# An attention and FFN kernel in split fp32: q and k laid out turned by the host, raw words as the high part

## The chip, the cores and the metric

The kernel runs on one core of a Trainium2 chip. The metric is the device time of one execution in microseconds (us), the median of several runs. The engines are named as in the profile: PE is the matrix engine (PEld its weight loads), DVE the vector engine, ACT the scalar engine, POOL the general engine, SP the engine whose queue issues the DMA transfers.

## The reference

Block-sparse attention over 4 x 8 heads with 768 positions of 64 columns, and then an FFN over the 3072 tokens of 512 columns:

```
scores = (q @ k.T) / sqrt(D)            # per head, 768 x 768
mask   = |blk_i - blk_j| <= 1, first and last block rows and columns,
         and 3 sampled key blocks of 32 for each query block
attn   = softmax(where(mask, scores, -1e9));   x = attn @ v
h = x @ w_in;   g = h - tanh(h);   out = g @ w_out
```

All inputs and the output are fp32.

## The kernel before

Every fp32 operand of a product on PE is taken as a sum of two parts, a high part that PE multiplies exactly and a low part that is the difference. Two heads form a pair (pr = 0 to 15; head h is half j = h % 2 of pair h // 2). The operands of a pair lie in one of three slots in SBUF (slot = pr % 3), each 128 x 4 x 2 x 768 words: sA, sB, sC, sD for x = 0 to 3, and the two halves j. The rows of sA hold the high part of k and the block mask, sB the high part of q, the one-hot block rows and (row 88) the negated row maximum nm, sC the low and high part of k, sD the high and low part of q.

For a pair, `load` brings k, q and v (rawk, rawq, rawv, 384 KB each, two buffers each). `prep_qk` turns k, and then q, by six 128 x 128 transposes on PE (L198) into a PSUM buffer, copies the result as the high part with ACT (hik, hiq, L200) and subtracts on DVE for the low part (lok, loq, L201). hi and lo have one buffer each. `dist` brings them into the slot by twelve transfers of 192 KB (L213): half j = 0 and j = 1 of k high into sA and sC, k low into sC, q high into sB and sD, q low into sD. A transfer into half j may start when the head that used this half of the slot, three pairs earlier, has been read for the last time.

For each head there are six steps over blocks of 128. `smax` (sm, L255) takes an estimate of the scores of 128 queries and DVE reduces it to a maximum (mc, L259). `smax_fin` turns the maxima (pmt, L264), forms nm on DVE (L266) and sends it into sB. `qk_exp` forms the scores turned, 128 keys x 768 queries (st, L283 and L284), and ACT takes the exponential (pe, L287). `split` makes its fp16 high part (ph, ACT L297 or DVE L295) and low part (pl, POOL L299, one of twelve on DVE). `accum` multiplies them by the parts of v (av, L313, L321, L322, 36 products for two key blocks), `norm` divides (xq, L335) and `spill` stores a pair's x in DRAM. sm, st and the turned q and k share the three PSUM buffers of the pool `big`, in rotation.

All steps are put in a list of events with a time each (`at`), sorted by it, and emitted in that order; a scheduler with a model of the engines then sets the order in which each engine has its instructions, and the buffers set the waits. SP issues its transfers strictly in that order, at most eight under way. In the first 150 us three pairs of FFN weight blocks are also read and converted on DVE (L436, L439, L442). The FFN follows: x and the weights are split in the same way, `h` and `out` are products on PE.

Of the kernel before, what the change touches and what calls it, by code (L numbers as in the profile page):

```python
# [55 lines left out]
TQK, TV, TSM, LSP, LAV = -15.1, -5.6, -9.95, 2.1, 4.2  # L56
# [16 lines left out]


@with_exitstack
def attention_ffn(ctx, tc, q, k, v, samp, w_in, w_out, blocks, out):
    nc = tc.nc
    cst = ctx.enter_context(tc.tile_pool(name="cst", bufs=1))
    dpool = ctx.enter_context(tc.tile_pool(name="dpool", bufs=1, space=DRAM))
    xscr = [dpool.tile([P, T, DM], F32, name=f"xscr{b}") for b in range(B)]  # L80

    ident = cst.tile([P, P], F32, name="ident")
    make_identity(nc, ident)
    bias = [cst.tile([P, 1], F32, name=f"bias{i}") for i in range(2)]
    for x, val in zip(bias, (QB, THR2)):
        nc.vector.memset(x, val)

    slots = [cst.tile([P, 4, 2, S], F32R, name=f"slot{i}") for i in range(NSLOT)]
    wt = {(m, ft): dpool.tile([P, 512], F32, name=f"w{m}{ft}") for ft in range(NPRE) for m in "io"}
    part = [dpool.tile([P, DM], F32, name=f"part{j}") for j in range(CT)]  # L90
    f2 = ctx.enter_context(tc.tile_pool(name="f2", bufs=2))
    stage = [cst.tile([P, 1024], I32, name=f"stage{i}") for i in range(2)]
    ffn = FFN(tc, w_in, w_out, xscr, ident, bias, slots, wt, out, f2, part, stage)
    with ExitStack() as actx:
        big = actx.enter_context(tc.tile_pool(name="ps_big", bufs=3, space=PSUM))
        one = actx.enter_context(tc.tile_pool(name="ps_one", bufs=2, space=PSUM))
        ps = (
            lambda name: big.tile([P, 1024], F32, tag="big", name=name),
            lambda name: one.tile([P, 512], F32, tag="one", name=name),
        )  # L100
        ffn.big, ffn.one = ps
        attention(actx, tc, q, k, v, samp, w_in, w_out, blocks, xscr, ident, ps, slots, wt, f2, ffn)
    with ExitStack() as fctx:
        ffn.rest(fctx)


def attention(ctx, tc, q, k, v, samp, w_in, w_out, blocks, xscr, ident, ps, slots, wt, f2, ffn):
    nc = tc.nc
# [9 lines left out]
    loads = {}  # L118
# [16 lines left out]
    def after(n, d):  # L135
        for f in urgent[n]:
            tc.add_manual_dep(
                d.ins, f.ins.name, mybir.DependencyInfo(mybir.DependencyClass.NoSync, mybir.DependencyReason.DATA), reason="first pair"
            )

    def load(pr, which="kqv", first=None):
        r = loads.setdefault(pr, [])
        for nm, src in ((n, x) for n, x in (("k", k), ("q", q), ("v", v)) if n in which):
            t = p2.tile([P, S], F32, tag="raw" + nm, name=f"raw{nm}{pr}", bufs=2)
            d = nc.sync.dma_start(out=t, in_=src[pr])
            r.append(t)
            if pr <= 3 and first is not None:
                after(first, d)

    load(0, "kq")  # L150
# [38 lines left out]
    hl = {}  # L189
    sbs = {}  # L190

    def prep_qk(pr, nm):
        raw = loads[pr][0 if nm == "k" else 1]
        hi = p2.tile([P, S], F32R, tag="hi" + nm, name=f"hi{nm}{pr}", bufs=1)
        lo = p2.tile([P, S], F32R, tag="lo" + nm, name=f"lo{nm}{pr}", bufs=1)
        pt = big(f"pt{nm}{pr}")
        for t in range(T):
            nc.tensor.transpose(pt[:, t * P : (t + 1) * P], raw[:, t * P : (t + 1) * P], ident)  # L198
        ptv = pt[:, 0:S]
        nc.scalar.activation(out=hi, in_=ptv, func=AF.Copy)  # L200
        nc.vector.tensor_tensor(out=lo, in0=ptv, in1=hi.bitcast(F32), op=ALU.subtract)  # L201
        hl[pr, nm] = hi, lo

    def dist(pr, nm, part):
        s = pr % NSLOT
        hi, lo = hl[pr, nm]
        if nm == "k":
            to = ((sA, 0, hi),) if part == 0 else ((sC, 64, hi), (sC, 0, lo))
        else:
            to = ((sB, 0, hi),) if part == 0 else ((sD, 0, hi), (sD, 64, lo))  # L210
        for dst, r0, src in to:
            for j in range(2):
                d = nc.sync.dma_start(out=dst[s].bitcast(F32)[r0 : r0 + 64, j], in_=src.bitcast(F32)[64 * j : 64 * j + 64])  # L213
                if pr == 0:
                    urgent[part].append(d)

    def prep_v(pr):
        rv = loads[pr][2]
        vf = rv.rearrange("p (n d) -> p n d", d=D)
        am = p2.tile([P, 1], F32, tag="am", name=f"am{pr}")  # L220
        d = nc.vector.tensor_reduce(
            out=am, in_=rv, op=ALU.max, axis=AX.X, apply_absolute_value=True
        )
        if pr > 1:
            tc.add_manual_dep(
                d.ins, maxed[-1].ins.name, mybir.DependencyInfo(mybir.DependencyClass.NoSync, mybir.DependencyReason.DATA), reason="late"
            )
# [118 lines left out]
    def ramp(h, by):  # L346

        return by * max(0, 1 - (h - 1) / HR) if h else 0

    def at(time, f, *args):  # L350
        ev.append((time, len(ev), f, args))

    at(-17.0, fill, 0, sB, onehot)
    at(TQK + 0.3, fill, 0, sA, mask, 0)
    at(TQK + 0.9, load, 1, "kq", 0)
    at(TQK + 1.7, load, 0, "v", 1)
    for i in range(1, NSLOT):
        for dst, src in ((sB, onehot), (sA, mask)):
            at(TQK + TF * i, fill, i, dst, src, 1)
    for pr in range(NPAIR):  # L360
        t0 = 12 * pr
        tl = TSM + ramp(NMH - 1, RS) + 6 * NMH + 0.1 * pr
        tqk, tv = TQK + ramp(2 * pr, RQ), TV + ramp(2 * pr, RV)
        if pr == 1:
            at(tl, load, 1, "v", 2)
        elif pr:
            at(max(t0 - 30, tl), load, pr, "kqv", 2)
        for nm, dt in (("k", 0), ("q", 0.5)):
            at(t0 + tqk + dt, prep_qk, pr, nm)
# [28 lines left out]
    xa = x_parts(slots[(NPAIR - 3) % NSLOT].rearrange("p a j s -> p (a j s)"))  # L398

    def x_first(j):  # L400
        raw = p2.tile([P, DM], F32, tag="raw" + "kq"[j % 2], name=f"xn0_{j}", bufs=2)
        nc.sync.dma_start(out=raw, in_=xscr[0][:, j, :])
        if j % 2 == 0:
            xa.append(big(f"xt0_{j}"))
        pt = xa[-1][:, j % 2 * 512 : j % 2 * 512 + 512]
        split_x(nc, raw, pt, xa[0][:, :, j * P : (j + 1) * P], xa[1][:, :, j * P : (j + 1) * P], ident)

    for j in range(CT):
        at(X0 + DX * j, x_first, j)
# [38 lines left out]
def split_x(nc, src, pt, xh, xl, ident):  # L448

    for c in range(NCT):  # L450
        nc.tensor.transpose(pt[:, c * P : (c + 1) * P], src[:, c * P : (c + 1) * P], ident)  # L451
    ptv = pt.rearrange("p (c n) -> p c n", c=NCT)
    nc.scalar.activation(out=xh, in_=ptv, func=AF.Copy)
    nc.vector.tensor_tensor(out=xl, in0=ptv, in1=xh.bitcast(F32), op=ALU.subtract)
# [230 lines left out]
```

## Time and profile before

| | |
|---|---|
| runs, us | 983.65, 980.24, 983.49; median 983.49 |
| span of the profiled execution, us | 983.2 (its own time is not listed apart) |
| busy: PE, DVE, ACT, POOL | 94%, 75%, 64%, 47% |
| transfers over the span | 99.78 MB, mean 101 GB/s |
| attention, about | 0 to 450 us |
| FFN, about | 450 to 983 us |

The page has each engine's busy time, the span in 40 slices with the busy share in tenths (PEclk is the granted clock of PE in tenths of full), the chain of work that ended last, and the costliest groups of instructions with what released them. Rows of single instructions give the start, the duration, the engine, the line, and in brackets how long the engine was idle ahead and what it waited for. The chain of waits gives start, duration and what was running.

### The profile page before, as it was taken

The page shows a single profiled execution, that of the slowest core. Times are in us where ns is not written, and L with a number is a line of the kernel's source. Part 1 is how long each engine was busy: PE and PEld are TensorE (multiplying, and loading weights), DVE is VectorE, ACT ScalarE, POOL GpSimd, SP SyncE. Part 2 cuts the span into 40 slices and gives each one's busy share as a digit, 9 for nine tenths or more (in the row PEclk, how much of TensorE's full clock was granted, in tenths as well). Part 3 has the DMA queues.
Part 4 walks back from the last instruction along what each step waited for, and adds up shares of the span by engine and source line. Part 5 has one row for each costly group of instructions (what it writes and reads, how often), then busy time and mean ns, then how long its engine had stood idle before and what let it go on. Part 6 is the DMA issues. An engine that isn't in the chain of part 4 may idle for free.

```text
span 983.2 us, 18548 instructions
## 1 busy us (share of the span) xinstructions
PE 922.6 (94%) x7264; PEld 771.1 (78%) x7264; DVE 733.4 (75%) x1119; ACT 629.7 (64%) x943; POOL 458.3 (47%) x308
## 2 busy tenths in 40 slices
PE   5788999999999999888999999999999999999997
PEld 3577788887888878767788888888888888888885
DVE  4589888887887878859999876765676666566664
ACT  1476888888888878656666665555555465555553
POOL 1365877777777777754445422222222222222221
PEclk9698999999999999898999999999999999999999
DMA  8796777676676667114451220210020000001001
GB/s 231 185 274 190 195 175 175 162 174 162 168 173 162 162 161 189 45 48 157 148 168 50 65 76 11 97 33 12 1 75 1 1 33 11 1 1 44 1 1 43
DMA packets 56263, 99.78 MB, mean 101 GB/s; under 512 B 6008, under 2 KB 26680, under 8 KB 56176
## 3 DMA queue, kind: packets, MB, share of 16 engines
q1 hardware_dynamic: 56176, 98.60, 37.0%
q8 instruction: 57, 0.93, 0.4%
q14 instruction: 30, 0.25, 0.1%
HBM read 44.64 MB, written 15.20 MB: 61 GB/s over the span
## 4 chain that ended last, share of the span: by engine, by line
PE 77%; ACT 6%; DMA 5%; DVE 5%; issue 3%; SPq 1%; POOL 1%; ACTq 0%; POOLq 0%; DVEq 0%
PE pf L537 25%; PE pf L569 8%; PE pf L570 8%; PE pf L571 8%; PE st L283 6%; PE st L284 5%; PE sm L255 5%; ACT pe L287 3%; PE av L313 2%; PE av L321 2%; PE av L322 2%; DMA slot<-lok 2%; DMA slot<-nm 2%; DVE mc L259 1%; PE pf L451 1%
## 5 line engine op out<-in xcount | busy, mean ns | idle before, releaser
L299 POOL TENSOR_TENSOR pl<-pe,ph 128x768 f16<-128x768 f32 x173 | 290.0, 1692 | 130.5 <-ACT ph L297 67.5
L560 POOL TENSOR_TENSOR gl<-t,gh 128x512 fp32r<-128x512 f32 x96 | 124.0, 1292 | 358.4 <-ACT gh L559 307.0
L259 DVE TENSOR_REDUCE mc<-sm 128x1 f32<-128x768 f32 x192 | 181.0, 951 | 53.1 <-PE sm L255 49.2
L287 ACT ACTIVATE pe<-st 128x768 f32<-128x768 f32 x192 | 154.1, 805 | 78.4 <-PE st L284 68.5
L283 PE MATMUL st<-slot 128*128 128x512 f32 (+1 forms) x384 | 146.4, 382 | 17.1 <-ACT pe L287 13.4
L552 DVE TENSOR_TENSOR t<-t,pf 128x512 f32<-128x512 f32 x94 | 64.5, 686 | 123.3 <-ACT t L546 123.2
L559 ACT ACTIVATE gh<-t 128x512 fp32r<-128x512 f32 x96 | 60.6, 632 | 120.2 <-DVE t L556 120.2
L297 ACT ACTIVATE ph<-pe 128x768 f16<-128x768 f32 x154 | 130.0, 844 | 4.7
L284 PE MATMUL st<-slot 89*128 89x512 f32 (+1 forms) x384 | 126.1, 349 | 1.0 <-DMA slot<-nm 1.0
L313 PE MATMUL av<-vhl,ph 128*128 128x65 f16 x1152 | 120.7, 195 | 0.0
L322 PE MATMUL av<-vhl,pl 128*128 128x65 f16 x1152 | 119.6, 194 | 0.9 <-POOL pl L299 0.9
L255 PE MATMUL sm<-slot 88*128 88x512 f32 (+1 forms) x384 | 111.1, 376 | 9.6 <-DMA slot<-hiq 7.0
L321 PE MATMUL av<-vhl,ph 128*128 128x64 f16 x1152 | 119.7, 196 | 0.0
L313 PEld LDWEIGHTS <-ph 128*128 128x128 f16 x1152 | 106.6, 97 | 13.6 <-issue 12.9
L322 PEld LDWEIGHTS <-pl 128*128 128x128 f16 x1152 | 107.9, 100 | 3.0 <-issue 1.5
L321 PEld LDWEIGHTS <-ph 128*128 128x128 f16 x1152 | 107.9, 98 | 0.7 <-issue 0.5
L544 ACT ACTIVATE u<-pf 128x512 f32<-128x512 f32 x94 | 56.2, 598 | 80.5 <-PE pf L537 80.2
L283 PEld LDWEIGHTS st<-slot 128*128 128x128 f32 x384 | 74.9, 195 | 35.1 <-ACT pe L287 18.5
L284 PEld LDWEIGHTS st<-slot 89*128 89x128 f32 x384 | 75.5, 197 | 11.2 <-DMA slot<-nm 2.2
L255 PEld LDWEIGHTS sm<-slot 88*128 88x128 f32 x384 | 62.6, 202 | 17.0 <-DMA slot<-mk 6.3
L570 PE MATMUL pf<-wx,gh 128*128 128x512 f32 x192 | 74.7, 389 | 0.0
L569 PE MATMUL pf<-wx,gh 128*128 128x512 f32 x192 | 74.7, 389 | 0.0
(123 smaller groups left out, 1962.8 us busy)
## 6 DMA issues: line engine op xcount, KB each, us to landing
slot<-hik SPq DMA_DIRECT2D x64, 192.0 KB
slot<-hiq SPq DMA_DIRECT2D x64, 192.0 KB
stage<-w_in SPq DMA_DIRECT2D x13, 512.0 KB
stage<-w_out SPq DMA_DIRECT2D x13, 512.0 KB
rawk<-k SPq DMA_DIRECT2D x16, 384.0 KB
rawq<-q SPq DMA_DIRECT2D x16, 384.0 KB
slot<-lok SPq DMA_DIRECT2D x32, 192.0 KB
slot<-loq SPq DMA_DIRECT2D x32, 192.0 KB
```

The source lines that it names most:

```text
L255: nc.tensor.matmul(pm[:, c], lhsT=sB[s][0:88, j, t * P : (t + 1) * P], rhs=sA[s][0:88, j, c], start=True, stop=True)
L259: maxed.append(nc.vector.tensor_reduce(out=mcs[h][:, t : t + 1], in_=pm[:, 0:S], op=ALU.max, axis=AX.X))
L283: ms.append(nc.tensor.matmul(st[:, c], lhsT=sC[s][:, j, kc], rhs=sD[s][:, j, c], start=True, stop=False))
L284: ms.append(nc.tensor.matmul(st[:, c], lhsT=sA[s][0:89, j, kc], rhs=sB[s][0:89, j, c], start=False, stop=True))
L287: nc.scalar.activation(out=pe, in_=st[:, 0:S], func=AF.Exp, scale=0.125)
L299: d = eng.tensor_tensor(out=pl, in0=pe, in1=ph, op=ALU.subtract)
L313: m = nc.tensor.matmul(o[:, t, :], lhsT=ph[:, c], rhs=vv[:, 0:65], start=(kt == 0 and t == 0), stop=False, skip_group_check=True)
L321: nc.tensor.matmul(o[:, t, 0:64], lhsT=ph[:, c], rhs=vv[:, 65:129], start=False, stop=False, skip_group_check=True)
L322: m = nc.tensor.matmul(o[:, t, :], lhsT=pl[:, c], rhs=vv[:, 0:65], start=False, stop=last, skip_group_check=True)
L537: nc.tensor.matmul(h, lhsT=w[:, cc], rhs=x[:, c, :], start=(k == 0), stop=(k == 3 * NCT - 1))
L569: nc.tensor.matmul(o, lhsT=gh[:, c], rhs=wo[0][ft], start=(ft == f0), stop=False)
L570: nc.tensor.matmul(o, lhsT=gh[:, c], rhs=wo[1][ft], start=False, stop=False)
```

## The change

The host lays out k and q of a pair turned and side by side, in one array of 16 x 128 x 1536 (row 64 j + d, column 768 x + position, x = 0 for k). One load (rawx, 768 KB, two buffers) takes the place of two. The transposes and the copies on ACT go. The high parts go into the slots straight from rawx, as raw words. For the low part DVE forms the words with the last 12 bits cleared (hi, L196, 128 x 1536) and subtracts these from the raw words (lo, L197, 128 x 1536), each with one buffer. The twelve transfers of a pair into the slot remain (now L210). The times of the events are altered so that the transfers of the high parts stand ahead of `prep_qk`. Four tiles of x at the start of the FFN take the buffers of rawv.

```diff
 def load(pr, which="kqv", first=None):
-    r = loads.setdefault(pr, [])
-    for nm, src in ((n, x) for n, x in (("k", k), ("q", q), ("v", v)) if n in which):
-        t = p2.tile([P, S], F32, tag="raw" + nm, name=f"raw{nm}{pr}", bufs=2)
-        d = nc.sync.dma_start(out=t, in_=src[pr])
+    for nm, src, n in (("x", kq, 2 * S), ("v", v, S)):
+        if nm in which:
+            t = p2.tile([P, n], F32, tag="raw" + nm, name=f"raw{nm}{pr}", bufs=2)
+            d = nc.sync.dma_start(out=t, in_=src[pr])
...
-def prep_qk(pr, nm):
-    raw = loads[pr][0 if nm == "k" else 1]
-    hi = p2.tile([P, S], F32R, tag="hi" + nm, name=f"hi{nm}{pr}", bufs=1)
-    lo = p2.tile([P, S], F32R, tag="lo" + nm, name=f"lo{nm}{pr}", bufs=1)
-    pt = big(f"pt{nm}{pr}")
-    for t in range(T):
-        nc.tensor.transpose(pt[:, t * P : (t + 1) * P], raw[:, t * P : (t + 1) * P], ident)
-    ptv = pt[:, 0:S]
-    nc.scalar.activation(out=hi, in_=ptv, func=AF.Copy)
-    nc.vector.tensor_tensor(out=lo, in0=ptv, in1=hi.bitcast(F32), op=ALU.subtract)
-    hl[pr, nm] = hi, lo
+def prep_qk(pr):
+    raw = loads[pr, "x"]
+    hi = p2.tile([P, 2 * S], I32, tag="hi", name=f"hi{pr}", bufs=1)
+    lo = p2.tile([P, 2 * S], F32, tag="lo", name=f"lo{pr}", bufs=1)
+    nc.vector.tensor_scalar(out=hi, in0=raw.bitcast(I32), scalar1=-4096, scalar2=None, op0=ALU.bitwise_and)
+    nc.vector.tensor_tensor(out=lo, in0=raw, in1=hi.bitcast(F32), op=ALU.subtract)
+    hl[pr] = lo
...
-    hi, lo = hl[pr, nm]
+    x = 0 if nm == "k" else 1
+    hi, lo = (a[:, x * S : (x + 1) * S] for a in (loads[pr, "x"], hl.get(pr, loads[pr, "x"])))
...
-        at(max(t0 - 30, tl), load, pr, "kqv", 2)
-    for nm, dt in (("k", 0), ("q", 0.5)):
-        at(t0 + tqk + dt, prep_qk, pr, nm)
-        at(t0 + tqk + dt + 0.01, dist, pr, nm, 0)
+        at(max(t0 - 30, tl), load, pr, "xv", 2)
+    for nm, dt in (("k", 0), ("q", 0.1)):
+        at(t0 + tqk + dt, dist, pr, nm, 0)
         at(t0 + tqk + 1.1 + dt, dist, pr, nm, 1)
+    at(t0 + tqk + 0.2, prep_qk, pr)
...
-    raw = p2.tile([P, DM], F32, tag="raw" + "kq"[j % 2], name=f"xn0_{j}", bufs=2)
+    raw = p2.tile([P, DM], F32, tag="rawv", name=f"xn0_{j}", bufs=2)
...
-    "q": pairs(inputs["q"], 0, 2, 3, 1, 4),
-    "k": pairs(inputs["k"], 0, 2, 3, 1, 4),
+    "kq": np.concatenate([pairs(inputs[n], 0, 1, 4, 3, 2) for n in "kq"], axis=2),
```

The change also moves instructions. In the rows that follow a name's first number is its pair (hik, lok, hiq, loq, rawx, lo, hi, rawv, xq), its head (nm, mc, av) or head and step (sm23_1); "waits" names what a row waits for: landed transfers (DMAHW) or an engine's progress.

SP at the start, before, from the fills of slots 1 and 2 to the second nm:

```order
L185 DMA slot2_75<-mk_125 24x2x768
L267 DMA slot0_73<-nm0_204 1x6x128
L213 DMA slot1_74<-hik1_226 64x768 x3
L213 DMA slot1_74<-hiq1_243 64x768 x2
L213 DMA slot1_74<-hik1_226 64x768
L213 DMA slot1_74<-lok1_227 64x768 x2
L213 DMA slot1_74<-hiq1_243 64x768 x2
L213 DMA slot1_74<-loq1_244 64x768 x2
L267 DMA slot0_73<-nm1_303 1x6x128
```

The same place now:

```order
L185 DMA slot2_75<-mk_123 24x2x768
L210 DMA slot1_74<-rawx1_139 64x768 x6
L210 DMA slot1_74<-lo1_213 64x768 x2
L210 DMA slot1_74<-rawx1_139 64x768 x2
L210 DMA slot1_74<-lo1_213 64x768 x2
L264 DMA slot0_73<-nm0_182 1x6x128
L264 DMA slot0_73<-nm1_263 1x6x128
```

nm0 stood ahead of the twelve transfers of pair 1 and now stands behind them.

DVE in the steady stretch, before, around the low parts of pair 12 (beside the maxima of head 23):

```order
L259 TENSOR_REDUCE mc23_5223<-sm23_1_5252 128x1
L201 TENSOR_TENSOR lok12_5233<-ptk12_5234,hik12_5232 128x768
L241 SCALAR_TENSOR_TENSOR vhl2_105<-rawv11_4186,sb11_5154,vhl2_105 128x12x64
L331 SCALAR_TENSOR_TENSOR rs20_5297<-av20_5092,sb10_4679 128x6
L334 RECIPROCAL rs20_5297<-rs20_5297 128x6
L259 TENSOR_REDUCE mc23_5223<-sm23_2_5325 128x1
L335 TENSOR_TENSOR xq10_5296<-av20_5092,rs20_5297 128x6x64
L201 TENSOR_TENSOR loq12_5302<-ptq12_5303,hiq12_5301 128x768
```

Now, some steps further, at the turn from head 23 to head 24:

```order
L256 TENSOR_REDUCE mc23_4979<-sm23_4_5134 128x1
L256 TENSOR_REDUCE mc23_4979<-sm23_5_5149 128x1
L197 TENSOR_TENSOR lo14_5911<-rawx14_5337,hi14_5910 128x1536
L256 TENSOR_REDUCE mc24_5205<-sm24_0_5206 128x1
L263 TENSOR_SCALAR nm23_5159<-pmt23_5157 6x128
L256 TENSOR_REDUCE mc24_5205<-sm24_1_5221 128x1
L196 TENSOR_SCALAR hi15_6358<-rawx15_5794 128x1536
```

Beside the maxima of heads 23 and 24 stand the low part of pair 14 and the mask of pair 15, two pairs further than before.

SP in the steady stretch, before, the end of pair 11's transfers and the start of pair 12's:

```order
L213 DMA slot2_75<-loq11_4827 64x768 [waits DMAHW2_49,DVE_49]
L213 DMA slot2_75<-loq11_4827 64x768 [waits DMAHW3_49]
L145 DMA rawq13_5131<-q 128x768 [waits DMAHW4_49,PE_49]
L267 DMA slot1_74<-nm21_4951 1x6x128 [waits DMAHW5_49,DVE_49]
L341 DMA xscr2_62<-xq9_4821 768x1x128 [waits DMAHW6_49,DVE_49]
L145 DMA rawk14_5599<-k 128x768 [waits DMAHW7_49,PE_49]
L267 DMA slot2_75<-nm22_5177 1x6x128 [waits DMAHW0_49,DVE_49]
L213 DMA slot0_73<-hik12_5232 64x768 [waits DMAHW1_49,Activation_49]
```

The same queue now, rows 237 to 245, the half j = 1 of pair 13:

```order
L210 DMA slot1_74<-rawx13_4887 64x768 [waits DMAHW5_49,PE_49]
L210 DMA slot1_74<-rawx13_4887 64x768 [waits DMAHW6_49,PE_49]
L210 DMA slot1_74<-rawx13_4887 64x768 [waits DMAHW7_49]
L145 DMA rawv13_4889<-v 128x768 [waits DMAHW0_49,DVE_49]
L210 DMA slot1_74<-lo13_5456 64x768 [waits DMAHW1_49]
L210 DMA slot1_74<-rawx13_4887 64x768 [waits DMAHW2_49]
L210 DMA slot1_74<-lo13_5456 64x768 [waits DMAHW3_49]
L145 DMA rawx15_5794<-kq 128x1536 [waits DMAHW6_49,DMAHW5_49,DMAHW7_49,DMAHW4_49,DMAHW2_49]
L264 DMA slot2_75<-nm23_5159 1x6x128 [waits DVE_49]
```

The transfers used to wait for ACT or DVE to make their part; the high parts now wait for PE, whose last read of that half of the slot is st21_5, and the two of lo13 stand behind them.

More of the change, by code (lines that the diff above doesn't have):

```diff
@@ L75, in attention_ffn @@
 @with_exitstack
-def attention_ffn(ctx, tc, q, k, v, samp, w_in, w_out, blocks, out):
+def attention_ffn(ctx, tc, kq, v, samp, w_in, w_out, blocks, out):
     nc = tc.nc
@@ L101, in attention_ffn, with attention @@
         ffn.big, ffn.one = ps
-        attention(actx, tc, q, k, v, samp, w_in, w_out, blocks, xscr, ident, ps, slots, wt, f2, ffn)
+        attention(actx, tc, kq, v, samp, w_in, w_out, blocks, xscr, ident, ps, slots, wt, f2, ffn)
     with ExitStack() as fctx:
         ffn.rest(fctx)
-def attention(ctx, tc, q, k, v, samp, w_in, w_out, blocks, xscr, ident, ps, slots, wt, f2, ffn):
+def attention(ctx, tc, kq, v, samp, w_in, w_out, blocks, xscr, ident, ps, slots, wt, f2, ffn):
     nc = tc.nc
@@ L141, in load @@
     def load(pr, which="kqv", first=None):
-        r = loads.setdefault(pr, [])
-        for nm, src in ((n, x) for n, x in (("k", k), ("q", q), ("v", v)) if n in which):
-            t = p2.tile([P, S], F32, tag="raw" + nm, name=f"raw{nm}{pr}", bufs=2)
-            d = nc.sync.dma_start(out=t, in_=src[pr])
[L146 to L150, printed above, removed]
+        for nm, src, n in (("x", kq, 2 * S), ("v", v, S)):
+            if nm in which:
+                t = p2.tile([P, n], F32, tag="raw" + nm, name=f"raw{nm}{pr}", bufs=2)
+                d = nc.sync.dma_start(out=t, in_=src[pr])
+                loads[pr, nm] = t
+                if pr <= 3 and first is not None:
+                    after(first, d)
+    load(0, "x")
     def setup():
@@ L212, in dist @@
             for j in range(2):
-                d = nc.sync.dma_start(out=dst[s].bitcast(F32)[r0 : r0 + 64, j], in_=src.bitcast(F32)[64 * j : 64 * j + 64])
+                d = nc.sync.dma_start(out=dst[s].bitcast(F32)[r0 : r0 + 64, j], in_=src[64 * j : 64 * j + 64])
                 if pr == 0:
@@ L217, in prep_v @@
     def prep_v(pr):
-        rv = loads[pr][2]
+        rv = loads[pr, "v"]
         vf = rv.rearrange("p (n d) -> p n d", d=D)
@@ L354, in attention @@
     at(TQK + 0.3, fill, 0, sA, mask, 0)
-    at(TQK + 0.9, load, 1, "kq", 0)
+    at(TQK + 0.9, load, 1, "x", 0)
     at(TQK + 1.7, load, 0, "v", 1)
```

## The prediction

> **What bounds the kernel now.** I read the first lines of the page, then the table of busy time by stretches of the span, then the groups of instructions in the steady stretch, then single rows. The page says that TensorE sets the pace:
>
> ```profile
> span 983.2 us, 18548 instructions
> PE 922.6 (94%) x7264; PEld 771.1 (78%) x7264; DVE 733.4 (75%) x1119; ACT 629.7 (64%) x943; POOL 458.3 (47%) x308
> PE   5788999999999999888999999999999999999997
> PEclk9698999999999999898999999999999999999999
> DMA  8796777676676667114451220210020000001001
> ```
>
> The stretches (columns: PE, PEld, DVE, ACT, POOL busy, each with its count, then granted clock, DMA share, GB/s) show four stages: a start in which the DMA is full, a ramp in which DVE also converts weights, a steady run of head pairs, a passage into the FFN, and the FFN, which the change leaves as it is.
>
> ```profile
> 0.00:40.00 40.00, 21.10 (x67) 15.62 (x68) 19.01 (x34) 10.08 (x12) 7.91 (x11) 0.83 0.89 217
> 40.00:107.30 67.30, 59.73 (x712) 50.31 (x711) 58.63 (x87) 45.99 (x58) 46.29 (x27) 0.92 0.77 224
> 107.30:393.30 286.00, 271.38 (x3610) 233.71 (x3608) 234.48 (x360) 237.48 (x299) 216.41 (x133) 1.00 0.69 170
> 450.00:983.20 533.20, 525.79 (x2350) 433.31 (x2348) 379.34 (x579) 302.61 (x526) 153.48 (x120) 1.00 0.14 45
> ```
>
> In the steady stretch, grouped by instruction (busy us, mean ns, idle ahead of it):
>
> ```profile
> L299 POOL TENSOR_TENSOR pl<-pe,ph 128x768 f16<-128x768 f32 x133 | 217.8, 1654 | 69.6 <-ACT ph L297 24.1 <-PE av L322 20.8 <-issue 18.5
> L283 PE MATMUL st<-slot 128*128 128x512 f32 (+1 forms) x288 | 107.3, 372 | 10.9 <-ACT pe L287 10.9
> L299 DVE TENSOR_TENSOR pl<-pe,ph 128x768 f16<-128x768 f32 x12 | 18.3, 1528 | 1.8 <-ACT ph L297 1.0
> L295 DVE CAST ph<-pe 128x768 f16<-128x768 f32 x24 | 15.7, 656 | 0.0
> L201 DVE TENSOR_TENSOR lok<-ptk,hik 128x768 fp32r<-128x768 f32 x12 | 11.4, 947 | 0.0
> L198 PE MATMUL ptq<-ident,rawq 128*128 128x128 f32 x72 | 10.5, 282 | 1.0 <-DVE lok L201 1.0
> L198 PE MATMUL ptk<-ident,rawk 128*128 128x128 f32 x72 | 9.9, 273 | 0.0
> ```
>
> The 72 transposes of ptk are 12 pairs at 6, so the period of a pair is 286.00 / 12 = 23.83 us. Transposes are 20.4 / 12 = 1.7 us of busy time in it, and PE idles 14.6 / 12 = 1.2 us, of which 0.9 is the wait of st for the exponential. PE without transposes is busy (271.38 - 20.4) / 12 = 20.9 us.
>
> **What goes away.** Per pair 12 transposes on PE, two copies on ACT and two subtractions on DVE (1.9 us). The saving on PE can be built up from the starts of three st tiles:
>
> ```profile
> 258.06 0.50 PE L283 MATMUL st<-slot 128*128 128x512 f32 x1 [0.94 <-ACT pe L287]
> 260.35 0.48 PE L283 MATMUL st<-slot 128*128 128x512 f32 x1
> 261.50 0.40 PE L283 MATMUL st<-slot 128*128 128x512 f32 x1
> ```
>
> One key tile with the products of two probability tiles behind it takes 2.29 us, one without takes 1.15, so such a group of products is 1.14. Six of each are 20.6 us a pair; the transposed maxima and the v scale add about 0.5: 21.1 us when nothing waits. So up to 23.83 - 21.1 = 2.7 us a pair lie on PE's own path and can go. They go only if nothing else makes PE wait.
>
> **What comes: two DVE instructions of 1536 columns.** The mask is one source by a constant. The nearest row is the weight conversion's first step:
>
> ```profile
> L436 DVE TENSOR_SCALAR cvti<-rawi 128x512 int32<-128x512 int32 x3 | 1.3, 418 | 2.6 <-DMA rawi<-w_in 2.6
> ```
>
> Three times 418 is 1.25 us; two of the casts above (656) are 1.31, so the mask is 1.0 to 1.3. The subtraction reads two SBUF tensors: two of L201 give 1.89, two of DVE's own pl (1528, beside POOL's pl) 3.06. I take 1.8, nearest to the same operation in L201, and keep 3.06 as the end. DVE is busy 234.48 / 12 = 19.5 us a period now; 2.8 (at most 4.4) in place of 1.9 makes that 20.4 (at most 22): as busy time it costs nothing.
>
> **What moves: the low part waits for its own transfers.** This is the term that decides. Both kernels have one low buffer. In the new order (rows of DVE and SP shown with the change) lo14 stands on DVE ahead of the reduction of sm24_0, and may not be written before lo13's second half has left for slot1. Those transfers (SP rows 241 and 243) stand behind the two of row 237 and 238 that wait for PE to finish with slot1, which is the end of st21_5; call that T. Before, each low part sat behind its own transposes about one pair later, when the transfers of the pair ahead had long landed (L201 shows 0.0 idle).
>
> From T the queue issues seven transfers: four of raw words, rawv, two of lo; rawv has twice the size, so eight units of 192 KB. What they take is seen in pieces of the chain of waits:
>
> ```profile
> 301.59 0.53 SPq L213
> 302.17 2.51 DMA slot<-hik
> 307.89 4.42 DMA slot<-lok
> 314.09 4.88 DMA slot<-nm
> ```
>
> A first transfer lands 0.53 + 0.05 + 2.51 = 3.1 us after its issue begins. A later one of a series shows 4.42 of its own. The rate is 170 GB/s at a share of 0.69, so 246 at full share, 0.8 us per 192 KB: the last lands between T + 3.1 + 7 x 0.8 = T + 8.7 and, with gaps between transfers, about T + 10. I take T + 9.5. Then lo (1.8) and the reduction (0.95, the size of L201's row) end at T + 12.2.
>
> PE from T has three groups of products (3.4), four key tiles (4.6) and one more sm (0.35) until st22_4, which takes the third rotating buffer and so waits for the reduction of sm24_0: T + 8.4. The stall is 12.2 - 8.4 = 3.8 us, between 3.0 and 5.6 (T + 10, and lo at 3.06). I add 0.2 for lo beside POOL: a period of 21.1 + 4.0 = 25.1, against 23.83. It happens for lo6 to lo15: ten pairs, +13. The cover that a wait on DVE had before, its one pair of lead, is gone; the pl, cast and maxima behind lo on DVE wait with it, but PE waits first for the maximum.
>
> **Clock.** A gap of that length did not occur in the steady stretch of before. Where one of half its length occurred, the clock fell:
>
> ```profile
> 409.19 1.12 PE L451 MATMUL xt<-ident,xn 128*128 128x128 f32 x4 [1.96 <-DVE slot L454]
> 405.50:409.00 3.50, 1.73 (x24) 1.32 (x20) 3.50 (x4) 3.05 (x6) 3.50 (x3) 0.99 0.30 112
> 409.00:412.40 3.40, 3.21 (x13) 2.60 (x14) 3.40 (x5) 1.31 (x2) 2.90 (x3) 0.50 0.00 0
> 412.40:415.80 3.40, 3.40 (x42) 3.21 (x40) 1.09 (x2) 0.94 (x2) 2.96 (x2) 0.50 0.01 2
> ```
>
> After 1.96 us without a matmul the clock is 0.50 for two stretches of 3.4 us. Each stretch at half clock does half the work, so it loses 1.7 us; a drop costs 1.7 to 3.4, and none if the gap misses. With one drop in most pairs I take 2 us a pair: +20, ends 0 and 34.
> By the Trainium skill (TensorE: Matmul & The Clock Gate, "Part 1: The HAM clock gate") the gate watches a free-running window of some 3.4 us and throttles after one idle window. The 3.4 us stretches agree, the row of 1.96 us does not fit a window that must be idle throughout. If it had to be, a gap of 3.8 us would hold such a window in about (3.8 - 3.4) / 3.4, one time in eight, and this term would be +3 instead of +20, the sum 1013: that is the second rival below.
>
> **Start.** The DMA is full from 0 to 40 us (0.89, 217 GB/s), so bytes ahead in the queue are time. Two rows of PE and SP, and three pieces of the chain of waits:
>
> ```profile
> 14.20 6.50 PE L255 MATMUL sm<-slot 88*128 88x512 f32 x16 [5.94 <-DMA slot<-hiq]
> 25.10 0.73 SPq L267 DMA_DIRECT2D slot<-nm  x1
> 32.20 0.80 PE st L284
> 13.69 8.72 DMA slot<-lok
> 25.10 7.05 DMA slot<-nm
> ```
>
> Before, the first st with its maximum starts at 32.20, when nm0 has landed; nm0 is issued ahead of pair 1's twelve transfers. Now it stands behind them: 12 x 0.197 = 2.36 MB at 0.217 MB/us is +10.9. Since the last eight transfers are still on their way when a later one is issued, not all of it counts: I take +9, ends 6 and 12.
>
> **Ramp (40 to 107).** DVE is busy 58.63 of 67.3 us with conversions. Here the preparation of pairs 2 to 5 stands where that of pairs 2 and 3 stood: 4 x 2.8 - 2 x 1.9 = +7.4 on a nearly full engine, and lo4 and lo5 already wait as above, against transposes saved there. I take +6, ends 0 and 12.
>
> **End.** The last pairs have no preparation: one period of 21.1 instead of 23.83, -2.7; the first x tiles take the buffers of rawv in place of rawk and rawq, at most +1: -2.
>
> **Sum.** 983.2 + 9 + 6 + 13 + 20 - 2 = 1029.2; the profiled execution is 0.3 below the median of the runs, so 1029.5, rounded 1029.
>
> **Rivals.**
> (a) The other side, PE gets free. If the transfers land early enough for lo to be done by the time PE arrives, that is by T + 8.4 - 2.75 = T + 5.65, there is no stall, and the next limit is POOL with DVE's two-input work: 217.8 / 12 = 18.15 a pair, and 1.53 + 1.8 + 1.0 of DVE on top if they exclude each other, 22.5. The period falls by 1.3 over 12 pairs: 983 - 16 + 9 = 976. For it speaks the 0.9 us of idle time and the 1.7 us of transposes; against it, eight units would have to move in 2.5 us after the first landed.
> By the Trainium skill (SBUF — State Buffer, "Who interferes with whom") a DVE operation with two SBUF inputs and a GpSimd operation that reads SBUF exclude each other; DVE's pl at 1528 against L201's 947 for the same size agrees.
> (b) The stall comes, the clock holds: 1029 - 17 to 20, about 1011.
> (c) The stall is half as long (transfers land at T + 7.5 since nothing else is in the queue): 23 a pair, -8, start and ramp +15, end -2, clock +2: about 990, and within 0.5% of before at the near edge of its ends.
> (d) A second wait follows. The x load (SP row 244) waits for transfers of the same series and nm23 stands behind it; it lands about T + 13, nm about T + 15, needed at about T + 16 with the stall. If it is late by 2 us a pair: +20, 1050.
> (e) The change does not remove what it names, because the transposes were hidden: PE at 94% and 0.0 idle ahead of ptk speak against it; it would make the slower forecasts worse by some 10.
>
> **Chances.** What a measurement of this kernel can tell from no change is about 0.5%, 5 us. Forecast (stall with clock drops, 1015 to 1045) 0.45; (b) 0.22; (c) 0.12, half of it within 0.5%; (d) with (e) 0.12; (a) 0.09, nearly all faster. So faster 0.08, same 0.07, slower 0.85. The range takes in (b), (d) and the upper half of (c): 990 to 1060.
>
> **What will show it.** Right: the group of L197 with some 3 us idle each, released by DMA slot<-lo; st (L280) idle after the reduction of sm (L256), 3 to 4 us ten times; granted clock under 0.9 between 120 and 400 us; first st with its maximum at about 41 us; no group on L198 and a steady period of 25 to 28. Wrong: L197 without idle time, PE busy above 95% in the steady stretch, a period under 23.8. If lo's transfers are issued at T but land by T + 6, the price of a series is what I got wrong; if lo is waiting and PE is not, the rotation of buffers is.

## The result, and the profile after

The changed kernel takes 1038.4 us (1037.5 to 1045.4) where the kernel before takes 982.2: a ratio of 1.059, interval 1.055 to 1.063. The forecast was 1029 in a range of 990 to 1060. The profiled execution took 1037.5 us, its span is 1035.8 (the span, from the first to the last instruction, is some 2 us shorter than the time).

The first lines of its page, and its busy time in two of the stretches used before (PE, PEld, DVE, ACT, POOL busy, granted clock, DMA share, GB/s):

```profile
span 1035.8 us, 18012 instructions
PE 921.5 (89%) x7072; PEld 765.5 (74%) x7072; DVE 762.3 (74%) x1119; ACT 605.2 (58%) x911; POOL 474.8 (46%) x308
PE   0687788878899888988899999999999999999997
PEclk9997799889988898999899999999999999999999
...
40.00:107.30 67.30, 51.19 (x509) 41.66 (x510) 50.93 (x69) 35.08 (x45) 39.28 (x21) 0.85 0.84 228
107.30:393.30 286.00, 239.71 (x3019) 204.22 (x3018) 228.34 (x315) 191.29 (x240) 202.94 (x116) 0.90 0.59 147
```

PE's 922.6 us of busy time became 921.5 although 192 of its matmuls are gone: the transposes were saved and given back at a lower clock (0.90 where it was 1.00). The rest is idle time: 14.6 us idle of 286 in the old steady stretch became 46.3. Two groups in it and two waits name the place:

```profile
L197 DVE TENSOR_TENSOR lo<-rawx,hi 128x1536 f32<-128x1536 f32 x11 | 29.1, 2641 | 30.3 <-DMA slot<-lo 26.4 <-issue 3.9
L280 PE MATMUL st<-slot 128*128 128x512 f32 x248 | 97.2, 392 | 34.6 <-DVE mc L256 33.2 <-ACT pe L284 1.3
...
PE st L280 <- DVE mc L256: 33.2, 12, 5.0
DVE lo L197 <- DMA slot<-lo: 26.4, 9, 4.4
```

One such wait in single rows: SP's issues (first and last of the series and rawv), the piece of the chain in which the last transfer of the series is under way, DVE, and PE.

```profile
245.69 1.76 SPq L210 DMA_DIRECT2D slot<-rawx  x3
247.55 0.54 SPq L145 DMA_DIRECT2D rawv<-v  x1
...
249.69 1.47 SPq L210 DMA_DIRECT2D slot<-lo  x1
...
249.69 5.54 DMA slot<-lo
...
255.35 1.97 DVE L197 TENSOR_TENSOR lo<-rawx,hi 128x1536 f32<-128x1536 f32 x1 [3.54 <-DMA slot<-lo]
257.24 0.94 DVE L256 TENSOR_REDUCE mc<-sm 128x1 f32<-128x768 f32 x1
...
258.24 0.50 PE L280 MATMUL st<-slot 128*128 128x512 f32 x1 [3.40 <-DVE mc L256]
```

The series begins at 245.69 when PE is done with the slot and its last transfer lands at 249.69 + 5.54 = 255.23, 9.5 us later. Then come lo, the maximum behind it, and st, after 3.40 us in which PE did nothing. There are nine gaps of this kind between 170 and 394 us, one for each of lo7 to lo15: seven of 3.40 us and two of 5.0, 3.75 in the mean.

Where the 52.6 us between the two spans came from (the medians of the runs lie 56.2 apart), by the end of a head's work (xq on DVE; heads 3, 5, 23 and 31), after and then before:

```profile
126.29 0.54 DVE L332 TENSOR_TENSOR xq<-av,rs 128x384 f32<-128x384 f32 x1
155.59 0.54 DVE L332 TENSOR_TENSOR xq<-av,rs 128x384 f32<-128x384 f32 x1
397.12 0.55 DVE L332 TENSOR_TENSOR xq<-av,rs 128x384 f32<-128x384 f32 x1
485.85 0.55 DVE L332 TENSOR_TENSOR xq<-av,rs 128x384 f32<-128x384 f32 x1
...
100.30 0.54 DVE L335 TENSOR_TENSOR xq<-av,rs 128x384 f32<-128x384 f32 x1
125.34 0.56 DVE L335 TENSOR_TENSOR xq<-av,rs 128x384 f32<-128x384 f32 x1
339.48 0.56 DVE L335 TENSOR_TENSOR xq<-av,rs 128x384 f32<-128x384 f32 x1
435.92 0.55 DVE L335 TENSOR_TENSOR xq<-av,rs 128x384 f32<-128x384 f32 x1
```

And the start, three rows of PE and SP after:

```profile
26.10 4.55 PE L252 MATMUL sm<-slot 88*128 88x512 f32 x11 [26.10 <-DMA slot<-mk]
39.74 0.76 SPq L264 DMA_DIRECT2D slot<-nm  x1
43.91 0.80 PE L281 MATMUL st<-slot 89*128 89x512 f32 x1 [5.08 <-DMA slot<-nm]
```

| stretch | forecast | measured |
|---|---|---|
| start, to the first st with its maximum | +9 | 43.91 - 32.20 = +11.7 |
| ramp, from there to head 5 | +9 | 30.25 - 11.7 = +18.5 |
| steady, heads 5 to 23 (9 pairs) | +30 | 241.53 - 214.14 = +27.4 |
| last pairs, heads 23 to 31 | -2 | 88.73 - 96.44 = -7.7 |
| FFN | 0 | 549.95 - 547.28 = +2.7 |

(The forecast of 33 for the ten stalls of lo6 to lo15 is shown for the nine that lie in the steady stretch. That of lo6, 3 us, lies ahead of the end of head 5 and is added to the 6 of the ramp.)

### The profile page after: what moved, and what is told of

Its sections match the earlier page's. It is cut to its first block, busy times and chain, and to the rows that moved or that the text cites. A ratio compares the mean times of both kernels' runs of the same rounds, so it can differ in the third digit from the quotient of the medians.

```text
span 1035.8 us, 18012 instructions
## 1 busy us (share of the span) xinstructions
PE 921.5 (89%) x7072; PEld 765.5 (74%) x7072; DVE 762.3 (74%) x1119; ACT 605.2 (58%) x911; POOL 474.8 (46%) x308
## 4 chain that ended last, share of the span: by engine, by line
PE 66%; DMA 15%; DVE 10%; issue 5%; ACT 2%; SPq 2%; POOL 0%; DVEq 0%; ACTq 0%; POOLq 0%
PE pf L534 23%; PE pf L566 8%; PE pf L567 8%; PE pf L568 7%; DMA slot<-lo 6%; PE st L280 5%; PE st L281 4%; PE sm L252 4%; DMA slot<-rawx 4%; DVE mc L256 3%; DMA rawx<-kq 3%; PE av L310 2%; PE av L318 2%; PE av L319 2%; SPq L210 1%
## 5 line engine op out<-in xcount | busy, mean ns | idle before, releaser
L296 POOL TENSOR_TENSOR pl<-pe,ph 128x768 f16<-128x768 f32 x173 | 306.0, 1787 | 164.0 <-ACT ph L294 80.2
L280 PE MATMUL st<-slot 128*128 128x512 f32 (+1 forms) x384 | 151.8, 396 | 42.7 <-DVE mc L256 38.6
L252 PE MATMUL sm<-slot 88*128 88x512 f32 (+1 forms) x384 | 118.6, 396 | 34.8 <-DMA slot<-mk 26.1
L281 PE MATMUL st<-slot 89*128 89x512 f32 (+1 forms) x384 | 132.5, 365 | 7.5 <-DMA slot<-nm 7.5
L310 PE MATMUL av<-vhl,ph 128*128 128x65 f16 x1152 | 126.1, 198 | 2.4 <-DVE nm L263 1.9
L280 PEld LDWEIGHTS st<-slot 128*128 128x128 f32 x384 | 79.7, 208 | 64.4 <-DVE mc L256 43.4
L318 PE MATMUL av<-vhl,ph 128*128 128x64 f16 x1152 | 124.8, 199 | 0.0
L319 PE MATMUL av<-vhl,pl 128*128 128x65 f16 x1152 | 124.3, 197 | 0.0
L310 PEld LDWEIGHTS <-ph 128*128 128x128 f16 x1152 | 110.1, 100 | 15.0 <-issue 14.5
L318 PEld LDWEIGHTS <-ph 128*128 128x128 f16 x1152 | 111.2, 100 | 1.9 <-issue 1.7
L541 ACT ACTIVATE u<-pf 128x512 f32<-128x512 f32 x94 | 56.2, 598 | 79.0 <-PE pf L534 78.4
L281 PEld LDWEIGHTS st<-slot 89*128 89x128 f32 x384 | 80.1, 209 | 17.9 <-DMA slot<-nm 8.1
```

Of the source, the lines that this page charges most:

```text
L252: nc.tensor.matmul(pm[:, c], lhsT=sB[s][0:88, j, t * P : (t + 1) * P], rhs=sA[s][0:88, j, c], start=True, stop=True)
L280: ms.append(nc.tensor.matmul(st[:, c], lhsT=sC[s][:, j, kc], rhs=sD[s][:, j, c], start=True, stop=False))
L281: ms.append(nc.tensor.matmul(st[:, c], lhsT=sA[s][0:89, j, kc], rhs=sB[s][0:89, j, c], start=False, stop=True))
L296: d = eng.tensor_tensor(out=pl, in0=pe, in1=ph, op=ALU.subtract)
L310: m = nc.tensor.matmul(o[:, t, :], lhsT=ph[:, c], rhs=vv[:, 0:65], start=(kt == 0 and t == 0), stop=False, skip_group_check=True)
L318: nc.tensor.matmul(o[:, t, 0:64], lhsT=ph[:, c], rhs=vv[:, 65:129], start=False, stop=False, skip_group_check=True)
```

## The experiments

**The later place.** Mask and subtraction of a pair are tied on DVE behind the last maximum emitted before them.

```diff
+        d = nc.vector.tensor_scalar(out=hi, in0=raw.bitcast(I32), ...)
+        if pr > 1:
+            tc.add_manual_dep(d.ins, maxed[-1].ins.name, ...)      # an order on DVE, no wait
```

> The changed kernel with one edit: the mask and the subtraction of a pair (from pair 2 on) stand on DVE behind the last maximum emitted before them, so some two pairs later than the scheduler put them; work and buffers are the same. Theory (the wait of lo for its own transfers stalls PE through the maximum queued behind it): lo has no idle time of more than 0.5 us, the gaps of 3.4 us ahead of st go, the granted clock from 150 to 390 us is above 0.97, the period of a pair falls from about 26.5 to 21.3 to 22.5, and the time to 965 to 990 (start still 11 us late). Rival (the two DVE instructions of 1536 columns beside POOL are the cost, wherever they stand): period 25 or more, 1025 to 1038. Rival (the transposes were hidden, so nothing is gained once the wait is gone): period 23.5 to 24, about 1000.

Measured: 1020.9 us (ratio to before 1.038, 1.035 to 1.040). The wait is gone, and with it the gaps of 3.4 us and a part of the drop of the clock, but the period fell only to 25.2. Groups from 107 to 393 us, the windows row of 190 to 390 us, and a row of PE:

```profile
L201 DVE TENSOR_TENSOR lo<-rawx,hi 128x1536 f32<-128x1536 f32 x11 | 32.6, 2967 | 0.0
L196 DVE TENSOR_SCALAR hi<-rawx 128x1536 int32<-128x1536 int32 x11 | 18.7, 1697 | 0.0
...
190.00:390.00 200.00, 177.18 (x2304) 150.11 (x2304) 177.91 (x239) 148.01 (x184) 151.73 (x87) 0.97 0.61 155
...
259.70 0.62 PE L256 MATMUL sm<-slot 88*128 88x512 f32 x2 [1.05 <-DVE mc L260]
```

The subtraction without idle time, with the same work at another place, shows that its wait was that for its own transfers. At this place the two instructions take 4.7 us, in the forecast 2.8, and sm now waits about 1 us at a time for maxima behind them. The clock is 0.96 from 150 to 390 us, where the theory said above 0.97 and the changed kernel has 0.91. The theory holds for the gaps and the first rival for the period (25 or more); the time lies between the two, and neither range took it in.

**The start.** Pair 1's transfers behind nm0, mk built ahead of the first mask.

```diff
+                elif pr == 1:
+                    after(2, d)
...
+        if pr == 0:
+            tc.add_manual_dep(d.ins, built[0].ins.name, ...)
```

> The changed kernel with two orders at the start put back: the twelve transfers of pair 1 behind nm0, and the mask rows mk built on DVE ahead of the mask and subtraction of pair 0. Theory (bytes ahead of mk and nm0 in the queue are the loss at the start): the first sm at about 16 to 19 us instead of 26, the first st with its maximum at 31 to 35 instead of 43.9, and the time 8 to 12 below the changed kernel, 1026 to 1030. Rival (the queue is full until about 100 us, so a transfer put ahead delays another one, and the ramp gives it back): the first st earlier as above, but the time within 4 of 1038.

Measured: 1028.9 us, 9.5 under the changed kernel. Two rows of PE and the end of head 5:

```profile
18.04 3.90 PE L259 MATMUL sm<-slot 88*128 88x512 f32 x10 [18.04 <-DMA slot<-mk]
34.69 0.80 PE L288 MATMUL st<-slot 89*128 89x512 f32 x1 [0.17 <-DMA slot<-nm]
...
144.17 0.55 DVE L339 TENSOR_TENSOR xq<-av,rs 128x384 f32<-128x384 f32 x1
```

The first st came 9.2 us earlier and the time followed, as the theory said: nothing was given back. The two orders were put back together, so their shares are not separated. Head 5 ends 18.8 us later than before although the start is only 2.5 us late, so the loss of the ramp is its own. In the later place, where the first st with its maximum was at 40.71 us (8.5 late), head 5 ended at 143.17, 17.8 late: the ramp's loss is 9.3 there, half of 18.5. The other half thus hangs on the same early place.

**Two buffers for lo.** The mask is written into lo, which leaves room for a second buffer.

```diff
-        hi = p2.tile([P, 2 * S], I32, tag="hi", name=f"hi{pr}", bufs=1)
-        lo = p2.tile([P, 2 * S], F32, tag="lo", name=f"lo{pr}", bufs=1)
+        lo = p2.tile([P, 2 * S], F32, tag="lo", name=f"lo{pr}", bufs=2)
...
```

> The changed kernel with the mask written into lo and subtracted there, so that lo has two buffers in the same space. Theory (lo waits for the transfers of the lo that had its buffer): the wait is one pair shorter, but the scheduler puts mask and subtraction one pair earlier as well, behind the second maximum of the next head; the wait then ends about a step after that maximum, the gaps shrink from 3.4 to under 2 us, the clock is mostly full, and the time is 985 to 1015. Rival (a second buffer takes the wait away altogether): as with the later place, 965 to 985. Rival (the DVE work itself): no change, 1030 to 1040.

Measured: 1036.6 us, no change within 2 us, and neither theory's reason. Two waits from 107 to 393 us:

```profile
DVE lo L195 <- DMA rawx<-kq: 41.4, 9, 5.6
PE sm L251 <- DVE mc L255: 28.8, 18, 4.3
```

The mask, which now bears the name lo, waits for its load (DMA rawx<-kq), 4.6 us a time, and the load is issued behind the same series of transfers that wait for PE. That is the load that rival (d) named, with the first wait taken away. Between these two edits it was DVE's instruction that had to move, not the buffer.

**The clock.** Fifteen products of 128 x 128 x 120 into unused columns fill the gap.

```diff
+        if kt == T - 1 and h % 2 and 5 <= h <= 23:
+            for _ in range(15):
+                m = nc.tensor.matmul(avt[h][:, 390:510], lhsT=ident, rhs=ident[:, 0:120], ...)
```

> The changed kernel with 15 products of 128 x 128 x 120 (unused columns of the accumulator) on PE after the last product of heads 5, 7 to 23, just where PE waits for the maximum behind lo: about 3.2 us of work in a gap of 3.4. Theory (part of the loss is the half clock that follows each gap): the granted clock between 150 and 390 us rises from 0.9 to above 0.97, the period falls by 1.3 to 2 us, the time falls to 1018 to 1028. Rival (the half clock costs nothing, since PE would only wait longer for the maximum): the clock rises, the time stays at 1034 to 1042. Rival (the wait is not a fixed time after the slot is free, so that the filler adds up): 1060 to 1070.

Measured: 1027.4 us, 11 under the changed kernel. The windows row of 150 to 390 us, with the filler and then without:

```profile
150.00:390.00 240.00, 234.82 (x3004) 202.81 (x3001) 201.70 (x280) 168.88 (x212) 179.74 (x102) 1.00 0.59 150
...
150.00:390.00 240.00, 205.55 (x2617) 176.87 (x2618) 188.97 (x269) 164.07 (x206) 170.25 (x100) 0.91 0.59 146
```

PE is busy for 29 us more in these 240 (the filler alone for 35.9), and the kernel is faster: the half clock after the gaps cost some 11 us. The theory holds for the clock and the time. The period, heads 5 to 23, fell from 26.8 to 25.7, so by 1.1, less than the 1.3 to 2 that was expected.

**The layout alone, in the kernel before.** q and k turned by the host, the high part by an ACT copy, the low part by two subtractions, order as before.

```diff
-            nc.tensor.transpose(pt[:, t * P : (t + 1) * P], raw[:, t * P : (t + 1) * P], ident)
...
+        d = nc.scalar.activation(out=hi, in_=raw, func=AF.Copy)
+        d = nc.vector.tensor_tensor(out=lo, in0=raw, in1=hi.bitcast(F32), op=ALU.subtract)
```

> The kernel before with the layout alone: q and k turned by the host, no transposes, high part by an ACT copy and low part by one DVE subtraction of 128x768 for k and one for q, as before but from SBUF; transfers, buffers and times of the events as before, the preparation held on ACT and DVE behind the work that stands ahead of it in the list of events, pair 1's transfers behind nm0. Theory (the transposes are on PE's path, and what the change lost is order, not work): the period falls from 23.8 to 21.3 to 22.5, and the time to 955 to 970. Rival (subtractions of two SBUF operands beside POOL's pl delay DVE and POOL as much as PE gains): period 23 to 24, 972 to 985. Rival (the transposes were hidden): 980 to 986.

Measured: 985.4 us, ratio 1.003 (1.001 to 1.005). The period is 23.3 us. Groups, the windows row and one row of PE:

```profile
L202 DVE TENSOR_TENSOR loq<-rawq,hiq 128x768 fp32r<-128x768 f32 x12 | 14.0, 1167 | 0.3 <-issue 0.3
107.30:393.30 286.00, 263.00 (x3531) 224.19 (x3527) 253.28 (x369) 239.67 (x306) 224.07 (x135) 0.99 0.68 172
...
257.95 0.61 PE L262 MATMUL sm<-slot 88*128 88x512 f32 x2 [1.26 <-DVE mc L266]
```

Of the 2.7 us a pair that the transposes could give, 0.5 are left. PE waits for a maximum in each pair, and DVE's busy time rose from 234.5 to 253.3 in the same stretch. The first rival (23 to 24) holds for the period, and the time lies at the upper end of its range. The time also lies in the range of the second rival, but the waits speak against hidden transposes: with them gone PE's busy time fell from 271.4 to 263.0 us in this stretch, and PE now waits 21.8 us for maxima where the kernel before shows no such wait. In the two profiled executions the layout alone is 4.1 us shorter (span 979.1 against 983.2); the medians have it 3.2 us longer, so the half microsecond a pair does not show in the time.

**Halves, earlier and spread.** Mask and subtraction in halves of 768, moved five and two steps earlier, start put back.

```diff
-        at(t0 + tqk + 0.2, prep_qk, pr)
+            at(t0 + tqk + dl, prep_qk, pr, nm)      # dl = -5.0 for k, -2.0 for q
```

> The changed kernel with the two orders at the start put back, and mask and subtraction in halves of 128x768, k's five steps and q's two steps earlier in the list of events than the single ones of the run with the later place, each behind the last maximum emitted before. Theory (in the later place mask and subtraction, 4.7 us in one piece beside the v low part, a cast and pl, made the maximum of sm late; spread out they fit): period 22 to 23.3, gaps ahead of sm under 0.6 us, clock above 0.98, time 965 to 985. Rival (DVE and POOL take turns on the port, so the sum counts wherever the pieces stand): period 24.5 to 25.5, 1003 to 1014, that is the run with the later place less the start. Rival (a new wait for the transfers): L197 or the subtraction idle for a DMA, period above 24.

Measured: 1034.7 us, worse than the later place with the start put back would be. The theory falls; the third rival's kind of wait came, on nm. Pieces of the chain:

```profile
263.13 0.87 DVE mc L269
...
264.21 6.62 DMA slot<-nm
270.88 0.50 PE st L294
```

nm, a transfer of 3 KB, takes 6.6 us, with the load of x and lo's transfers issued just ahead of it. In the 286 us such waits for nm are 19.5 us of PE's idle time, waits of st for a maximum another 17.4.

**The same with the casts on ACT** (`PH_DVE = ()`).

> The run in halves with the two casts of ph per pair taken from DVE to ACT (1.3 us off DVE, 1.7 onto ACT). Theory (DVE is now the engine nearest to PE's 21.2 us a pair): the period falls by 0.3 to 1.0 against the run in halves, time 4 to 12 lower. Rival (PE sets the pace in the run in halves): within 3. Rival (ACT becomes the limit, since the exponential waits for its copies): 3 to 10 slower.

Measured: 1048.3 us, slower by 13.5, outside all three forecasts. It says little on DVE: nm makes st wait there too (27.0 us in the 286), and POOL waits for ACT's copies (73.2, against 49.3 in halves). The run is inconclusive.

**DVE's pl on POOL, in the layout alone** (`PL_DVE = ()`).

> The kernel of the layout alone with DVE's one pl in twelve given to POOL (1.7 us a pair off DVE, 1.65 onto POOL, which is busy 224 of 286 us). Theory (in the layout alone the maximum of sm comes late because DVE has the two subtractions, the v low part, a cast and pl in one stretch without a pause of 7 us beside the maxima): the gaps of 1.25 us ahead of sm go or halve, the period falls from 23.33 to 22.2 to 22.9, the time by 6 to 14 to about 970 to 978. Rival (POOL is as near to its limit): period 23.2 to 24, time within 4 or slower by up to 8.

Measured: 981.5 us, ratio 0.999 (0.997 to 1.001), 4 under the layout alone. The gaps of 1.25 us ahead of sm remained, and the period, heads 5 to 23, is 23.7: the rival's numbers. In the layout alone that pl starts at 261.22 us, behind the maximum that the sm of 257.95 waits for, so it was not pl that made that maximum late.

**Later low parts, in the layout alone.**

```diff
+            dl = dt + 3.5 * (1 + dt) if pr > 1 else dt
+            at(t0 + tqk + dl + 0.005, prep_lo, pr, nm)
```

> The kernel of the layout alone with the two subtractions 3.5 and 5 steps later in the list of events than the high parts, so that they stand beside the end of a head's maxima and the start of the next. Theory (the stretch is too full, not the engine: DVE is busy 20.7 of 23.3 us): gaps ahead of sm under 0.7 us, period 22 to 22.8, time 966 to 976. Rival (DVE's whole load with the delays on the port sets the pace wherever the pieces stand): period 23 to 23.5, time within 4 of the layout alone. Rival (nm waits in the queue behind the later transfers of lo): st waits for nm more than 0.5 us a pair, slower than the layout alone.

Measured: 975.4 us, ratio 0.9934 (0.9914 to 0.9954): faster than both kernels. The period is 23.0 us and steady, the clock 1.00. Groups:

```profile
L208 DVE TENSOR_TENSOR loq<-rawq,hiq 128x768 fp32r<-128x768 f32 x12 | 27.3, 2276 | 0.0
L208 DVE TENSOR_TENSOR lok<-rawk,hik 128x768 fp32r<-128x768 f32 x12 | 18.6, 1547 | 0.0
L311 DVE TENSOR_TENSOR pl<-pe,ph 128x768 f16<-128x768 f32 x12 | 11.3, 946 | 0.0
```

Three subtractions of the same size take 0.95, 1.55 and 2.28 us by their place. The time lies in the theory's range and the period (23.0) in the rival's: the place decides what a subtraction costs, and with DVE busy for 92% (263.9 of 286) PE still waits for maxima, 19.9 us in the 286, 1.7 a pair. The two profiled executions lie only 1.6 us apart (spans 979.1 and 977.5) where the medians lie 10 apart, so the profiles show only a part of the gain over the layout alone.

**The later place, the start, and DVE's pl on POOL, in the changed kernel.**

> The changed kernel with the later place, the two orders at the start put back, and DVE's pl given to POOL. Theory (in the later place DVE's burst is the limit, 25.2 us a pair; the start is 9 us by itself): the start and the place add up to 1011, and 1.8 us less in the burst takes 1 to 1.8 off the period, so 23.4 to 24.2 and 993 to 1001. Rival (the place of the burst matters but not its length, since the port is taken by POOL just as long): period 25, 1008 to 1014.

Measured: 1012.2 us. The start and the place add up as expected, to 1011, and with pl moved as well the time is no lower: the rival's range. Its reason is not shown by that, because the granted clock from 150 to 390 us is 0.90 where the later place had 0.96, which may have taken back what pl gave.

**Halves, later.** As the halves above, with 3.5 and 5.0 in place of -5.0 and -2.0.

> The changed kernel with the two orders at the start put back, and mask and subtraction in halves of 128x768 at about the place that the subtractions have in the run of the layout with later low parts (the end of a head's maxima); the high parts go into the slots as raw words. Against that run it has two masks a pair more on DVE and two copies less on ACT. Theory (place and length of DVE's burst are what was lost): no wait for nm over 0.5 us a pair, the granted clock above 0.97, period 23 to 24.3, time 980 to 998, so most of the change's loss is gone though all of its operations remain. Rival (raw words sent straight from the load bring a wait of their own, since the queue stands until PE is done with a slot): st waits for nm as in the halves placed earlier, period above 25, time above 1005.

Measured: 1056.8 us, the slowest of all, with a period of 28.9. The rival's numbers came (above 25, above 1005), but not its cause: st has no wait for nm there. DVE's rows in one pair, and PE's:

```profile
270.68 1.77 DVE L198 TENSOR_SCALAR hik<-rawx 128x768 int32<-128x768 int32 x1
273.23 1.13 DVE L198 TENSOR_SCALAR hiq<-rawx 128x768 int32<-128x768 int32 x1
274.29 2.40 DVE L207 TENSOR_TENSOR lok<-rawx,hik 128x768 f32<-128x768 f32 x1
276.61 2.39 DVE L207 TENSOR_TENSOR loq<-rawx,hiq 128x768 f32<-128x768 f32 x1
...
279.92 0.61 PE L265 MATMUL sm<-slot 88*128 88x512 f32 x2 [3.30 <-DVE mc L269]
```

7.7 us of DVE for what takes 1.9 in the kernel before (where ACT makes the high parts), most of it in one piece ahead of a maximum, and so a gap of 3.30 us, as long as the one in the changed kernel, with no wait for a transfer in it.

## Why the prediction was right

**The wait of lo for its own transfers: right in place, and in size partly by luck.** The later place takes it away with the same instructions: shown. T is the time at which PE is done with the slot, read here as the start of the series at SP. From there lo starts after 8.7 to 10.6 us in the nine stalls (9.7 in the one shown), 9.3 in the mean, where 9.5 was taken. The stall was 3.8 and is 3.75 in the mean. Two terms of that sum were off by about 0.8 us and cancelled: lo takes 2.68 us in these stalls, not 1.8, and PE runs dry at about T + 9.15 (258.24 - 3.40 - 245.69 in the rows above), not at T + 8.4. Nine such stalls came, not ten: PE's gap at lo6 was 1.84 us. The transposes did go from PE's path: at the end, where no pair is prepared any more, two pairs take 21.2 and 21.5 us, next to the 21.1 of the forecast. The forecast counted one such pair, so the last pairs give -7.7 against -2.

**The period: right as a sum, 27.1 forecast and 241.53 / 9 = 26.8 measured.** Its terms were not all right. The clock was put at 2.0 a pair and cost about 1.1 by the filler. Of the rest, 26.8 - 21.1 - 3.4 - 1.1 = 1.2, the two gaps of 5.0 us are 0.35; no run separates what is left. The whole came nearer than its parts, since they partly cancel: the ramp took 9 us more than forecast, the steady and the last pairs together 8 less. The 0.3 us at the end of the sum sets the span of 983.2 beside times, which lie some 2 us above their spans; it only carries the +46 over to the median of 983.49, so nothing hangs on it.

**The clock: the profile's row was the better guide.** By the Trainium skill (TensorE: Matmul & The Clock Gate, "Part 1: The HAM clock gate") the clock is halved after at least one idle window of about 3.4 us. For a gap of 3.8 us the forecast estimated from that one time in eight. Here is one gap and the stretches behind it:

```profile
198.00:202.75 4.75, 1.35 (x38) 1.16 (x37) 3.75 (x3) 1.98 (x3) 4.54 (x3) 0.84 0.53 171
202.75:207.60 4.85, 4.85 (x27) 4.06 (x28) 4.07 (x8) 1.97 (x3) 1.59 (x2) 0.50 0.08 19
207.60:211.00 3.40, 3.40 (x42) 2.88 (x40) 2.03 (x4) 1.97 (x3) 2.28 (x2) 0.94 0.97 211
```

All nine gaps of 3.4 us or more between 170 and 394 us were followed by half clock, so the second rival is out. In all thirteen traces, between 125 and 420 us, half clock set in during or within 3.5 us after every gap of 2.5 us or more; of eleven gaps of 1.7 to 2.3 us it did so for six (in the kernel before for the 1.96 us that the forecast shows, and not for 2.06 us ahead of 399.5 us). Gaps of about 1 us are not free of it either, as the 0.96 of the later place shows. The clock from 150 to 390 us, 0.91, just missed the sign that was named (under 0.9).

**The start: right, a little small.** 11.7 where 9 was taken and 10.9 counted; the fill of the mask rows behind the first lo, which the forecast's account of the start leaves out, held the first sm until 26.10.

**The ramp: the term that was mis-sized, +6 forecast (+9 with the stall of lo6) and +18.5 measured.** It was priced by 7.4 us more of DVE work; the waits of lo4 and lo5 were named and set against the transposes saved, without a price. Between the first st with its maximum and the end of head 3 (44 to 126 us, before 32 to 100) DVE is busy 12.3 us more than before and PE idle 10.3 us more. The later place takes 9.2 of the 18.5 away. How much of it is work on DVE and how much waiting is not separated.

**"As busy time it costs nothing": wrong.** lo was taken at 1.8 and is 2.64 (2.97 in the later place), near the far end of 3.06 that the row of DVE's own pl had given; the mask was 1.0 to 1.3 and is 1.06, or 1.70 where POOL is at work. In the stalls PE waits for the maximum behind lo, so lo's 0.9 us more lie on PE's path there. Without the wait the two instructions are the next limit: 25.2 us a pair, where rival (a) had put 22.5. So that rival was wrong by more than its condition: even with the wait gone the changed kernel would not have been faster.

**Rival (e)** is answered by the layout alone: the transposes were not hidden, but only 0.5 us of their 2.7 was free to take, because PE then waits for DVE's maxima.

## What to carry to other kernels

Where an engine's queue holds an instruction that waits for a buffer, look what stands behind it and who needs that: here a second buffer moved the wait to a load, and of the edits tried only another place for the instruction took it away. When work is taken off the busiest engine, price what the next one does at that spot beside its neighbours, from the row of the same operation under the same company, not from its busy share. A change of layout pays only as far as the work that stays has room: of 2.7 us a pair 0.5 came through, and 0.8 with the low parts placed where the maxima leave space.

## What the runs showed of the hardware

A DVE subtraction of 128x768 with both operands in SBUF took from 0.93 to 2.41 us in these runs, and the difference is POOL's pl beside it. Rows of POOL and DVE from the run with the later low parts show how:

```profile
258.69 1.66 POOL L311 TENSOR_TENSOR pl<-pe,ph 128x768 f16<-128x768 f32 x1 [0.49 <-PE sm L267]
259.61 1.56 DVE L208 TENSOR_TENSOR lok<-rawk,hik 128x768 fp32r<-128x768 f32 x1
261.09 0.94 DVE L311 TENSOR_TENSOR pl<-pe,ph 128x768 f16<-128x768 f32 x1
261.17 7.92 POOL L311 TENSOR_TENSOR pl<-pe,ph 128x768 f16<-128x768 f32 x4 [0.82 <-PE av L334]
```

lok starts while a pl of POOL runs, which ends at 260.35, and ends 0.82 us after that. The next subtraction on DVE starts 0.08 us ahead of POOL and takes 0.94; POOL's four take 7.92 there, where four of 1.65 would be 6.6. The one that starts first goes through and the other waits for its end. By the Trainium skill (SBUF — State Buffer, "Who interferes with whom") a DVE instruction with two SBUF inputs contends with a GpSimd instruction (POOL here) that reads SBUF, and whoever issues first gets the ports that they share for the whole instruction. These rows agree. DVE's subtraction in the kernel before, with one operand in PSUM, took 0.95 us in all of its 32 instances, with POOL's pl beside it or not.

So halving the instruction made it worse here: one subtraction of 1536 columns took 2.97 us in the later place, two of 768 took 2.40 + 2.39 in the later halves. In the rows of the halves each of the two starts while a pl of POOL runs (to 275.87 and to 278.18 us) and ends 0.82 us after it, so each waits anew.
